# fp32 weight loads on SyncE's queue with on-chip conversion, and a new loop order, in a windowed-attention and highway-FFN kernel

## The chip, the core and the metric

One core of a Trainium2 chip runs the whole kernel. The metric is the time of one execution on the device, in microseconds (us); lower is better. A profile describes one execution; its span is about 2 us shorter than that execution's time. Each variant was timed in alternation with the kernel before on the same chip. The chips differ from round to round, and the median of the kernel before with them (129.19 to 129.88 us), so variants of different rounds are compared by their ratio to it.

## The reference

Attention with 4 sink keys and a causal window of 128, then a highway layer over the concatenated heads (cut):

```python
# q, k, v: (4, 8, 768, 64) fp32, n_sink = 4, window = 128
scores = scale * np.matmul(q, k.transpose(0, 1, 3, 2))
keep = (pos[None, :] < n_sink) | ((rel >= 0) & (rel < window))
scores = np.where(keep, scores, -1000000000.0)
a = softmax(scores)                          # written out in the reference
x = (a @ v), heads joined                    # (3072, 512)
H = np.maximum(x @ w_h, 0.0)                 # w_h, w_t: (512, 512) fp32
T = 1.0 / (1.0 + np.exp(-(x @ w_t + b_t)))
out = T * H + (1.0 - T) * x                  # (3072, 512) fp32
```

## The kernel before

The 3072 tokens are 24 blocks of 128; six blocks make a sequence. For each block the kernel

- loads q, k and v with GpSimd's DMA queue, which casts fp32 to fp16 on the way (rows of 64 elements, so 1,024 packets of 128 bytes for each load),
- transposes q and k on TensorE (`pe_T`) and copies them to SBUF on ScalarE (`act_T`, tile `qk`),
- computes scores (`pe_S`), exponentials on ScalarE (`act_S`), masks on VectorE (`dve_mask`), the product with v (`pe_A`), its reciprocal and scaling on VectorE (`dve_rec`, `dve_x`),
- transposes x on TensorE (`pe_X`), copies it on ScalarE (`act_X`), and does the two FFN products (`pe_Mt` for t, `pe_Mh` for h), `act_u`, and three VectorE steps (`dve_d`, `dve_e`, `dve_o`), followed by the store.

Each engine works through its own instructions in program order, and waits on semaphores for the others. The loads at the head of the program:

```python
def load_w(w, sb):
    nc.gpsimd.dma_start(out=sb, in_=w.rearrange("(kc p) of -> p kc of", p=P))   # casts

with tc.manual_schedule(engines={ENG.Pool}):
    load_qk(0)
    # ... ident (cut)
    load_v(0)
    load_qk(1)
    # ... masks (cut)
    load_v(1)
    load_sink_v(0)
    load_w(moe_w_t, wt_sb)
    load_w(moe_w_h, wh_sb)
    # ... bm (cut)
    load_qk(2)
    load_v(2)
    load_qk(3)
```

The start and the loop (cut):

```python
if i == -2:
    warm_up(8); more_constants(); pe_T(0); act_T(0)
elif i == -1:
    pe_S(0, 0) ...; dve_mask(0, 0); dve_mask(0, 1)
    pe_T(1); act_T(1)
    pe_A(0); dve_rec(0); dve_x(0)
    pe_S(1, 0) ...; dve_mask(1, 0); dve_mask(1, 1)
    pe_X(0); act_X(0); spare(3)
    pe_A(1); dve_rec(1); dve_x(1) ...
elif i == 0:
    pe_Mt(0); act_u(0); pe_X(1); act_X(1); pe_Mt(1)
    pe_Mh(0); dve_d(0); act_u(1)
    pe_T(2); act_T(2)
    ...
else:                                   # the loop
    pe_T(i + 2); act_T(i + 2)
    dve_mask(i, 1); dve_e(i - 2)
    pe_S(i + 1, 0); pe_S(i + 1, 1)
    pe_X(i - 1); act_X(i - 1); act_S(i + 1, 0); dve_o(i - 2)
    pe_A(i); dve_rec(i); dve_x(i)
    # ... sink scores of every other block (cut)
    act_S(i + 1, 1)
    pe_Mh(i - 1); dve_d(i - 1); pe_Mt(i - 1); act_u(i - 1)
    dve_mask(i + 1, 0)
```

The PSUM tiles of `pe_T`, `pe_X`, `pe_Mt`, `pe_Mh` and the sink scores share two buffers in turn, so the order of these steps also decides who waits for whose buffer.

The softmax here doesn't subtract the row's maximum and nothing guards it: scores larger than these inputs give would overflow.

## Time and profile before

| | before |
|---|---|
| median of the runs | 129.77 us |
| span of the profiled run | 127.8 us |
| first qk copy (block 0) starts | 6.90 us |
| block 1's av product done | 15.23 us |
| block 4's av product done | 35.35 us |
| six blocks of the loop | 26.1 us |

"av product done" is read here, and everywhere below, as the start of the reciprocal that follows it on VectorE.

From the page of the kernel before: the head, and busy time of an engine with its share of the span and its count of instructions.

```profile
span 127.8 us, 3253 instructions
...
PE 110.1 (86%) x1315; PEld 67.9 (53%) x1315; DVE 101.8 (80%) x214; ACT 97.6 (76%) x129; POOL 74.9 (59%) x98
```

No engine is the bottleneck over the whole span, so the reading goes by stages. The chain of work that ended last, for the kernel before; columns are start, duration (us), and what it was:

```profile
7.71 0.57 POOL vd L127
8.28 0.76 POOL wt_sb L135
9.04 9.43 DMA wh_sb<-in_moe_w_h_dram
18.47 0.28 issue
18.75 0.87 POOL qsd L86
...
21.38 0.84 POOL qsd L86
22.22 6.38 DMA ksd<-in_k_dram
28.60 0.05 issue
28.64 0.41 PE tp L199 x4
...
69.86 1.04 PE hps L341 x4
70.89 0.22 PE tps L326
71.11 0.88 PE tps L328 x4
71.99 0.02 issue
72.01 0.60 ACT u L334
72.61 0.90 ACT qk L204
73.51 0.49 ACT xT L318
```

Up to 28.6 us the chain holds load issues and loads: the casting h load, then a k load behind it. After that it is a ring: h and t products on TensorE, then u, qk and xT on ScalarE, which the next h product needs. One turn is 4.2 us.

### The profile page before, as it was taken

The page shows a single profiled execution, that of the slowest core. Times are in us where ns is not written, and L with a number is a line of the kernel's source. Part 1 is how long each engine was busy: PE and PEld are TensorE (multiplying, and loading weights), DVE is VectorE, ACT ScalarE, POOL GpSimd, SP SyncE. Part 2 cuts the span into 40 slices and gives each one's busy share as a digit, 9 for nine tenths or more (in the row PEclk, how much of TensorE's full clock was granted, in tenths as well). Part 3 has the DMA queues.
Part 4 walks back from the last instruction along what each step waited for, and adds up shares of the span by engine and source line. Part 5 has one row for each costly group of instructions (what it writes and reads, how often), then busy time and mean ns, then how long its engine had stood idle before and what let it go on. Part 6 is the DMA issues. An engine that isn't in the chain of part 4 may idle for free.

```text
span 127.8 us, 3253 instructions
## 1 busy us (share of the span) xinstructions
PE 110.1 (86%) x1315; PEld 67.9 (53%) x1315; DVE 101.8 (80%) x214; ACT 97.6 (76%) x129; POOL 74.9 (59%) x98
## 2 busy tenths in 40 slices
PE   6758989569999899999998999999989999999620
PEld 2236434447755574586555656755655666564300
DVE  6544626495999898998998998989989999899760
ACT  4066435999897998998987989989969989893310
POOL 6999939999899989999999995005000000000000
PEclk9999999999999999999999999999999999999996
DMA  0999999999999999999999999922022202210222
GB/s 1 105 126 140 165 153 157 180 181 197 160 156 204 204 180 201 163 199 200 164 199 194 208 159 205 186 95 82 8 82 82 82 5 82 82 60 28 82 82 82
DMA packets 79728, 17.00 MB, mean 133 GB/s; under 512 B 75617, under 2 KB 76641, under 8 KB 79714
## 3 DMA queue, kind: packets, MB, share of 16 engines
q0 software_dynamic: 76256, 10.51, 122.6%
q1 hardware_dynamic: 3458, 6.30, 13.3%
q8 instruction: 10, 0.16, 0.5%
q14 instruction: 4, 0.03, 0.1%
HBM read 21.01 MB, written 6.29 MB: 214 GB/s over the span
## 4 chain that ended last, share of the span: by engine, by line
PE 39%; ACT 29%; DMA 12%; POOL 9%; DVE 6%; issue 3%; POOLq 0%; ACTq 0%
PE tps L328 14%; PE hps L341 11%; ACT qk L204 10%; DMA wh_sb<-in_moe_w_h_dram 7%; ACT u L334 6%; ACT e L252 6%; ACT xT L318 5%; DMA ksd<-in_k_dram 5%; PE tps L326 4%; POOL qsd L86 3%; PE sps L244 3%; PE av L280 2%; POOL ksd L87 2%; POOL v L94 2%; PE xtp L313 2%
## 5 line engine op out<-in xcount | busy, mean ns | idle before, releaser
L252 ACT ACTIVATE e<-sps,ebias 128x1024 f16<-128x1024 f32 (+1 forms) x48 | 48.6, 1054 | 1.8 <-PE sps L244 1.8
L263 DVE TENSOR_TENSOR e<-e,mask 128x1024 f16<-128x1024 f16 (+1 forms) x48 | 29.1, 640 | 4.7 <-ACT e L252 4.6
L204 ACT COPY qk<-tp 128x1024 f16<-128x1024 f16 x24 | 24.2, 1009 | 6.4 <-PE tp L199 6.4
L341 PE MATMUL hps<-wh_sb,xT 128*128 128x512 f16 x96 | 24.8, 380 | 3.4 <-ACT xT L318 2.9
L334 ACT ACTIVATE u<-tps 128x512 f16<-128x512 f32 x24 | 14.3, 597 | 16.0 <-PE tps L328 16.0
L328 PE MATMUL tps<-wt_sb,xT 128*128 128x512 f16 x96 | 25.0, 384 | 0.1
L86 POOL DMA_DIRECT2D qsd<-in_q_dram x24 | 22.4, 932 | 3.4 <-DMA wh_sb<-in_moe_w_h_dram 2.0
L94 POOL DMA_DIRECT2D v<-in_v_dram x24 | 22.3, 929 | 0.5 <-DVE dd L347 0.3
L347 DVE SCALAR_TENSOR_TENSOR dd<-hps,xh 128x512 f16<-128x512 f32 x24 | 16.6, 691 | 7.4 <-PE hps L341 5.7
L87 POOL DMA_DIRECT2D ksd<-in_k_dram x24 | 22.1, 920 | 0.5 <-PE tps L328 0.3
L353 DVE SCALAR_TENSOR_TENSOR ee<-u,dd 128x512 f16<-128x512 f16 x24 | 16.5, 689 | 3.5 <-ACT u L334 3.2
L280 PE MATMUL av<-v,e 128*128 128x66 f16 x352 | 17.7, 197 | 0.6 <-DVE e L263 0.5
L328 PEld LDWEIGHTS <-xT 128*128 128x128 f16 x96 | 9.4, 98 | 15.0 <-issue 4.1
L299 DVE TENSOR_TENSOR xh<-av,rec 128x512 f16<-128x512 f32 x24 | 16.6, 692 | 0.8
L359 DVE SCALAR_TENSOR_TENSOR otok<-xh,ee 128x512 f32<-128x512 f16 x24 | 16.6, 692 | 0.8
L280 PEld LDWEIGHTS <-e 128*128 128x128 f16 x352 | 15.2, 100 | 2.2 <-DVE e L263 1.9
L244 PE MATMUL sps<-qk 64*128 64x128 f16 x352 | 14.6, 223 | 1.5 <-ACT qk L204 1.5
L318 ACT COPY xT<-xtp 128x512 f16<-128x512 f16 x24 | 14.4, 598 | 0.4 <-PE xtp L313 0.3
L341 PEld LDWEIGHTS <-xT 128*128 128x128 f16 x96 | 7.9, 97 | 12.0 <-ACT xT L318 5.7
L244 PEld LDWEIGHTS <-qk 64*128 64x128 f16 x352 | 10.4, 97 | 4.8 <-ACT qk L204 1.4
L199 PE MATMUL tp<-ident,ksd 128*128 128x128 f16 x96 | 9.8, 227 | 1.7 <-DMA ksd<-in_k_dram 1.6
L197 PEld LDWEIGHTS <-qsd 128*128 128x128 f16 x96 | 7.2, 100 | 6.8 <-DMA qsd<-in_q_dram 2.2
(51 smaller groups left out, 100.2 us busy)
## 6 DMA issues: line engine op xcount, KB each, us to landing
out_dram<-otok SPq DMA_DIRECT2D x24, 256.0 KB, 4.5
qsd<-in_q_dram POOLq DMA_DIRECT2D x24, 128.0 KB, 6.5
ksd<-in_k_dram POOLq DMA_DIRECT2D x24, 128.0 KB, 6.5
v<-in_v_dram POOLq DMA_DIRECT2D x24, 128.0 KB, 6.7
wt_sb<-in_moe_w_t_dram POOLq DMA_DIRECT2D x1, 512.0 KB, 7.3
wh_sb<-in_moe_w_h_dram POOLq DMA_DIRECT2D x1, 512.0 KB, 9.4
vd<-in_v_dram POOLq DMA_DIRECT2D x4, 4.0 KB, 4.9
bt<-in_moe_b_t_dram SPq DMA_DIRECT2D x1, 2.0 KB
```

The source lines that it names most:

```text
L86: nc.gpsimd.dma_start(out=qsd, in_=q[b, :, rows, :].transpose([1, 0, 2]))
L87: nc.gpsimd.dma_start(out=ksd, in_=k[b, :, rows, :].transpose([1, 0, 2]))
L94: nc.gpsimd.dma_start(out=vt[:, :, 0:D], in_=v[b, :, rows, :].transpose([1, 0, 2]))
L204: nc.scalar.copy(out=qk, in_=tp_of.pop(n))
L244: nc.tensor.matmul(sps[:, hh, o:o + P], lhsT=kk[rows, hp, :], rhs=qT[rows, hp, :], start=True, stop=True)
L252: nc.scalar.activation(out=e.rearrange("p a b c d -> p a (b c d)"), in_=sps[:, :, 0:2 * np_ * P], func=AF.Exp, bias=ebias, scale=SCALE)
L263: nc.vector.tensor_tensor(out=ev, in0=ev, in1=m.unsqueeze(1).to_broadcast([P, 4, np_ * P]), op=ALU.mult)
L280: nc.tensor.matmul(av[:, g, 2 * hl + hh, 0:_AVN], lhsT=e[:, hh, hl, pc, :], rhs=vt[:, 65 * h:65 * h + _AVN], start=first, stop=False, skip ...
L318: nc.scalar.copy(out=xT, in_=xtp_of.pop(n))
L328: nc.tensor.matmul(tps, lhsT=xT[:, kc, :], rhs=wt_sb[:, kc, :], start=False, stop=(kc == NOC - 1))
L334: nc.scalar.activation(out=u, in_=t_of.pop(n), func=AF.Tanh)
L341: nc.tensor.matmul(hps, lhsT=xT[:, kc, :], rhs=wh_sb[:, kc, :], start=(kc == 0), stop=(kc == NOC - 1))
```

## The change

The intent, as the diff shows it: free GpSimd's queue of the weights, give the DMA engines large packets for them, convert on engines that wait at the start anyway, and open the ring by moving the x transpose to the head of the iteration. The diff, cut to its core:

```diff
-    vs_dn = [const.tile([NS4, D], FP16, ...) for i in range(2)]
+    vs_dn = [const.tile([NS4, D], FP32, ...) for i in range(B)]
+    w32 = {w: const.tile([P, NOC, DM], FP32, ...) for w in "th"}
-    with tc.manual_schedule(engines={ENG.Pool}):
+    with tc.manual_schedule(engines={ENG.Pool, ENG.SP}):
+        for w, src in (("t", moe_w_t), ("h", moe_w_h)):
+            nc.sync.dma_start(out=w32[w], in_=src.rearrange("(kc p) of -> p kc of", p=P))
+        nc.sync.dma_start(out=bt32, in_=moe_b_t.unsqueeze(0))
+        for b in range(B):
+            nc.sync.dma_start(out=vs_dn[b], in_=v[b, :, 0:NSINK, :])
         load_qk(0)
 ...
-        load_sink_v(0)
-        load_w(moe_w_t, wt_sb)
-        load_w(moe_w_h, wh_sb)
 ...
             if i == -2:
                 warm_up(8)
                 more_constants()
+                for kc in range(NOC):
+                    convert(nc.scalar, "t", kc)
                 pe_T(0)
                 act_T(0)
 ...
-                pe_T(1)
-                act_T(1)
                 pe_A(0)
                 dve_rec(0)
                 dve_x(0)
+                pe_T(1)
+                act_T(1)
 ...
+            elif i == 0:
+                pe_X(0)
+                act_X(0)
+                convert(nc.vector, "h", 0)
+                convert(nc.vector, "h", 1)
                 dve_mask(1, 0)
                 dve_mask(1, 1)
-                pe_X(0)
-                act_X(0)
-                spare(3)
+                convert(nc.vector, "h", 2)
+                convert(nc.vector, "h", 3)
+                pe_T(2)
+                act_T(2)
                 pe_A(1)
                 dve_rec(1)
                 dve_x(1)
+                pe_Mt(0)
+                act_u(0)
+                pe_Mh(0)
+                dve_d(0)
 ...
+            elif not late:                    # the new loop
+                (no sinks:) pe_X(i-1); act_X(i-1)      (sinks: act_sink(i))
+                dve_mask(i, 1)
+                pe_S(i+1, 0); act_S(i+1, 0); pe_S(i+1, 1)
+                dve_e(i-2)
+                (sinks:) pe_X(i-1); act_X(i-1)
+                pe_T(i+2); act_T(i+2)
+                dve_o(i-2)
+                pe_A(i); dve_rec(i)
+                dve_mask(i+1, 0); act_S(i+1, 1)
+                dve_x(i)
+                pe_Mh(i-1); dve_d(i-1); pe_Mt(i-1); act_u(i-1)
+                pe_sink(i+1)
```

The diff also moves the loads of blocks 10 and 11 by a step in GpSimd's queue. **T0**: the first qk copy (`act_T(0)`). **T1**: block 1's transposes, now behind block 0's av product instead of ahead of it.

More of the change, by code (lines that the diff above doesn't have):

```diff
@@ L113 @@
     vs_bd = [const.tile([P, H, 65], FP16, tag=f"vs{i}", name=f"vs{i}") for i in range(2)]
-    vs_dn = [const.tile([NS4, D], FP16, tag=f"vd{i}", name=f"vd{i}") for i in range(2)]
+    vs_dn = [const.tile([NS4, D], FP32, tag=f"vd{i}", name=f"vd{i}") for i in range(B)]
+    w32 = {w: const.tile([P, NOC, DM], FP32, tag=f"w32{w}", name=f"w32{w}") for w in "th"}
     es_t = [const.tile([P, 2, P], FP16, tag=f"es{i}", name=f"es{i}") for i in range(2)]
@@ L124 @@
             init_v(vt)
-    def load_sink_v(b):
-        nc.gpsimd.dma_start(out=vs_dn[b % 2], in_=v[b, :, 0:NSINK, :])
     def sink_v(b, eng):
         eng.tensor_tensor(
-            out=vs_bd[b % 2][0:NS4, :, 0:D], in0=vs_dn[b % 2].unsqueeze(1).to_broadcast([NS4, H, D]),
+            out=vs_bd[b % 2][0:NS4, :, 0:D], in0=vs_dn[b].unsqueeze(1).to_broadcast([NS4, H, D]),
             in1=bm[0:NS4, :].unsqueeze(2).to_broadcast([NS4, H, D]), op=ALU.mult)
-    def load_w(w, sb):
-        nc.gpsimd.dma_start(out=sb, in_=w.rearrange("(kc p) of -> p kc of", p=P))
-    with tc.manual_schedule(engines={ENG.Pool}):
+    with tc.manual_schedule(engines={ENG.Pool, ENG.SP}):
[4 more added lines that the diff above has]
+            nc.sync.dma_start(out=vs_dn[b], in_=v[b, :, 0:NSINK, :])
         load_qk(0)
@@ L162 @@
         load_qk(3)
-    nc.sync.dma_start(out=bt32, in_=moe_b_t.unsqueeze(0))
     def more_constants():
@@ L366, in lag @@
     def lag(n):
-        if n < 2:
-            return 1 - n
+        if n == 1:
+            return 0
         return 1 if n not in XBAR else 3 if n < LATE else 2
@@ L377, in spare, with convert @@
             nc.tensor.matmul(w, lhsT=warm[:, 0:P], rhs=warm, start=True, stop=True)
+    def convert(eng, w, kc):
+        sb = {"t": wt_sb, "h": wh_sb}[w]
+        if eng is nc.scalar:
+            eng.copy(out=sb[:, kc, :], in_=w32[w][:, kc, :])
+        else:
+            eng.tensor_copy(out=sb[:, kc, :], in_=w32[w][:, kc, :])
     with tc.manual_schedule(engines={ENG.PE, ENG.DVE, ENG.Activation, ENG.SP, ENG.Pool}):
         for i in range(-2, NB + 2):
-            ms = [m for m in range(2, NB) if m + lag(m) == i]
+            ms = [m for m in range(1, NB) if m + lag(m) == i]
             os_ = [m for m in range(1, NB) if m + lag(m) == i - 1]
+            late = len(XBAR) and i > XBAR[0]
             if i == -2:
@@ L411 @@
                 dve_x(1)
+                pe_Mt(0)
+                act_u(0)
+                pe_Mh(0)
+                dve_d(0)
                 sink_ones()
                 sink_v(0, nc.vector)
-            elif i == 0:
-                pe_Mt(0)
-                act_u(0)
+            elif i == 1:
                 pe_X(1)
                 act_X(1)
-                pe_Mt(1)
-                pe_Mh(0)
-                dve_d(0)
-                act_u(1)
-                pe_T(2)
-                act_T(2)
-                dve_e(0)
-                pe_Mh(1)
-                dve_o(0)
-                dve_d(1)
-            elif i == 1:
                 pe_S(2, 0)
                 act_S(2, 0)
-                dve_mask(2, 0)
+                dve_e(0)
                 pe_S(2, 1)
@@ L435 @@
                 act_T(3)
+                dve_o(0)
                 act_S(2, 1)
-                pe_sink(2)
-                act_sink(2)
-            else:
+                dve_mask(2, 0)
+                pe_Mh(1)
+                dve_d(1)
+                pe_Mt(1)
+                act_u(1)
+                dve_mask(2, 1)
+                pe_sink(2)
+            elif not late:
+                sk = has_sink(i)
+                x = on(i - 1) and i > 2
+                if x and not sk:
+                    pe_X(i - 1)
+                    act_X(i - 1)
+                if sk:
+                    act_sink(i)
+                if i > 2 and on(i):
+                    dve_mask(i, 1)
+                if on(i + 1):
+                    pe_S(i + 1, 0)
+                    act_S(i + 1, 0)
+                    pe_S(i + 1, 1)
+                for o in os_:
+                    dve_e(o)
+                if x and sk:
+                    pe_X(i - 1)
+                    act_X(i - 1)
                 if on(i + 2):
@@ L442 @@
                     act_T(i + 2)
-                if on(i):
-                    dve_mask(i, 1)
-                for o in os_:
-                    dve_e(o)
-                if on(i + 1):
-                    pe_S(i + 1, 0)
-                    pe_S(i + 1, 1)
-                if on(i - 1) and i - 1 not in XBAR and i - 1 > 1:
-                    pe_X(i - 1)
-                    act_X(i - 1)
-                if on(i + 1):
-                    act_S(i + 1, 0)
                 for o in os_:
@@ L459 @@
                     dve_rec(i)
+                if on(i + 1):
+                    dve_mask(i + 1, 0)
+                    act_S(i + 1, 1)
+                if on(i):
+                    dve_x(i)
+                if i in XBAR:
+                    sp_X(i)
+                for m in ms:
+                    pe_Mh(m)
+                    dve_d(m)
+                    pe_Mt(m)
+                    act_u(m)
+                if has_sink(i + 1):
+                    pe_sink(i + 1)
+            else:
+                if i == XBAR[0] + 1:
+                    dve_mask(i, 1)
+                    if has_sink(i):
+                        act_sink(i)
+                if on(i + 2):
+                    pe_T(i + 2)
+                    act_T(i + 2)
+                for o in os_:
+                    dve_e(o)
+                if on(i + 1):
+                    pe_S(i + 1, 0)
+                    act_S(i + 1, 0)
+                    pe_S(i + 1, 1)
+                if on(i - 1) and i - 1 not in XBAR:
+                    pe_X(i - 1)
+                    act_X(i - 1)
+                if on(i):
+                    pe_A(i)
+                    dve_rec(i)
+                for o in os_:
+                    dve_o(o)
+                if on(i):
                     dve_x(i)
@@ L474 @@
                     dve_mask(i + 1, 0)
+                    dve_mask(i + 1, 1)
             if on(i + 2) and (i + 2) % NSC == 0:
@@ L479 @@
                     sink_v(b, nc.gpsimd)
-                if b + 1 < B:
-                    load_sink_v(b + 1)
-            for n in {-2: range(3, AHEAD + 1), 0: [], 1: [10, 11]}.get(i, [i + 2 + AHEAD]):
+            for n in {-2: range(3, AHEAD + 1)}.get(i, [i + 2 + AHEAD]):
                 if n < NB:
```

## The prediction

> **What bounds the kernel now.** Two stages.
>
> *Start, 0 to 28.6 us: loads.* The chain of waits runs through GpSimd's DMA issues (0.9 us each), 9.43 us of the wh load, then 6.38 us of a k load. Only at 28.64 us can block 5 be transposed; later the chain holds no load. Beside the casting weight loads, q, k and v loads took 8.0 us to land (3.6 to 4.1 earlier); GpSimd once waited 2.03 us for wh.
>
> *Loop, 28.6 to 118 us: a ring through the engines.* In the timeline an iteration takes 4.20 us, or 4.67 with sink scores: 26.1 us per six blocks. The table of stretches has TensorE busy 24.9 of these, VectorE 23.9, ScalarE 23.8. The ring: TensorE's h and t matmuls (2.1 us), ScalarE's u, qk, xT (2.0), h again. So a perfect order would save at most about 1.2 us per six blocks, 3.6 in 18.
>
> **What the change does.** It removes two casting weight loads (1.5 us of GpSimd; about 7.7 us of DMA). It adds 2 MB of fp32 on SyncE's queue, four ScalarE conversions *ahead of the first qk copy*, four on VectorE where it is idle, and drops three spare matmuls.
>
> The Trainium skill, "DMA: Bandwidth & Descriptors" (queues, rings and completion order), says that each DMA engine takes turns between queues packet by packet. The trace agrees: during a store (25 to 26 us) the software queue moved 636 packets in 1 us instead of about 1,220, the store about 217 GB/s; alone, stores run near 400. Estimate: wt lands near 6.3 us, wh near 11; q and k of block 0 at 5.4 and 7 (before 4.96 and 6.26); k of block 5 near 22 instead of 28.6. Loads stop being the limit.
>
> But the conversions (estimate 4 x 0.5 us, from ScalarE's 128x512 copies) follow wt's landing: the first qk copy starts near 8.4 us instead of 6.90. Walking the new order from there with the trace's durations, block 4's av matmuls end at 34.8 to 36.5 us (before 35.3): early data is spent on a later, more serial start (block 1's transposes wait for block 0's av), partly at the cold matmul rate (427 ns per 128x512, not 216). Start: 0 to +1 us.
>
> *Loop.* The ScalarE ring opens: x is copied first, 2 us before h needs it. But dd now follows rec, mask and xh on VectorE, and the next x transpose needs the buffer that dd frees: 0.04+0.24+0.60+0.61+0.65 = 2.14 us after av, plus 2.04 us of TensorE = 4.18 us. Nearly the old period (4.63 with sink scores); only the half-size block of each sequence gets shorter, about 0.5 us. Over 18 iterations -1.5 us (range -4 to +1). Tail: unchanged within 0.4 us.
>
> Sum near -0.7; the walk leaves out slack that blocks lend each other, so -1.4.
>
> **Predicted: 128.3 us, range 125.3 to 131.0. Faster by over 2%: 0.31; within 2%: 0.58; slower by over 2%: 0.11.**
>
> **What shows it.** Right: weights land near 6 and 11 us; no load in the chain after 12 us; the qk copy starts at 8 to 9 us after four conversions; block 4's av ends near 35.5; iterations of 4.1 to 4.25 us with TensorE waiting for dd. Wrong: qk copy before 7.5 or after 10; average period still 4.35, or below 4.2.
>
> **What would make it wrong.** Weights starved by small packets (wt after 9 us), or delaying q and k; the matmul clock cold to 20 us or more; earlier masks letting all engines fill (period 4.15: about 126); conversions over 0.6 us.

## The result, and the profile after

| | before | after | difference |
|---|---|---|---|
| median of the runs | 129.77 us | 134.03 us | |
| ratio of the fast runs | | 1.034 (95%: 1.030 to 1.038) | slower |
| span of the profiled run | 127.8 us | 132.5 us | +4.7 |
| first qk copy starts (T0) | 6.90 | 11.81 | +4.9 |
| from T0 to block 1's av | 8.33 | 10.09 | +1.8 |
| from T0 to block 4's av | 20.12 | 18.12 | -2.0 |
| from block 4's av to block 22's (18 blocks) | 78.25 | 78.10 | -0.2 |
| from block 22's av to the end | 14.2 | 14.4 | +0.2 |

A ratio is the mean time of one kernel's fast runs over that of the other's of the same rounds, so it is not quite the ratio of the medians. The whole loss lies before block 4. The loop is as long as it was.

The same lines of the page of the changed kernel:

```profile
span 132.5 us, 3280 instructions
...
PE 109.2 (82%) x1312; PEld 68.2 (51%) x1312; DVE 102.3 (77%) x218; ACT 99.7 (75%) x133; POOL 70.6 (53%) x92
```

The chain that ended last, for the changed kernel, columns as before:

```profile
1.33 1.06 POOL qsd L86
2.39 8.72 DMA ksd<-in_k_dram
11.11 0.05 issue
11.16 0.62 PE tp L194 x4
11.78 0.02 issue
11.81 1.02 ACT qk L199
...
75.70 0.88 PE tps L323 x4
76.58 0.02 issue
76.60 0.25 ACT u L329
76.85 0.25 issue
77.09 0.58 ACT xT L313
77.67 1.02 ACT e L247
78.69 0.91 ACT qk L199
79.60 0.04 issue
79.64 0.38 PE tps L321
80.02 0.86 PE tps L323 x4
```

The start now hangs on the very first k load, which took 8.7 us to land where it took 3.8 before; the first q load took 9.0 us instead of 3.6. The view of the k tile for that load, before and after:

```profile
DMA to landing us min/median/max: 3.8/3.8/3.8
...
DMA to landing us min/median/max: 8.7/8.7/8.7
```

The ScalarE conversions, for which the prediction delayed T0, ran from 6.58 to 8.75 us, and ScalarE then waited 3 us more for k. What the DMA engines did meanwhile is in the DMA view of the changed kernel over four stretches, 3 to 4, 6 to 7, 8 to 9 and 10 to 11 us. q1 is SyncE's hardware queue (the weights), q0 GpSimd's software queue (q, k, v); after each name stand packets, MB and the packets' time as a share of 16 engines (over 100% where packets overlap).

```profile
q1 hardware_dynamic: 192, 0.39, 105.0%
...
q1 hardware_dynamic: 166, 0.34, 96.2%
q0 software_dynamic: 30, 0.00, 5.8%
...
q1 hardware_dynamic: 194, 0.23, 78.5%
q0 software_dynamic: 294, 0.04, 57.5%
...
q0 software_dynamic: 1228, 0.16, 243.4%
```

The first q load was issued by 2.4 us and needs 1,024 packets. While the weights were under way, it got almost none: its first packet moved at 5.98 us (3.09 in the kernel before), and by 9 us the software queue had moved 427. In the loop the ring closed again in another place: the t product needs the PSUM buffer that the qk copy frees, and on ScalarE the qk copy comes behind u, xT and one exponential. That turn is 4.32 us (75.70 to 80.02).

The table of stretches for the changed kernel, 8 to 28 us; per stretch the busy time of each engine with its count, then the granted TensorE clock, the DMA share and GB/s:

```profile
8.00:12.00 4.00, 1.22 (x8) 0.69 (x8) 0.41 (x1) 0.95 (x3) 0.00 (x0) 0.50 2.12 183
12.00:16.00 4.00, 1.92 (x23) 1.50 (x24) 1.29 (x4) 2.08 (x3) 3.00 (x6) 0.50 1.62 103
16.00:20.00 4.00, 2.79 (x33) 2.10 (x31) 2.19 (x4) 2.92 (x3) 4.00 (x6) 0.50 1.81 116
20.00:24.00 4.00, 3.62 (x23) 1.78 (x24) 2.54 (x5) 1.82 (x4) 4.00 (x5) 0.50 2.22 144
24.00:28.00 4.00, 3.43 (x37) 2.00 (x36) 2.81 (x7) 2.99 (x5) 4.00 (x6) 0.92 2.30 144
```

TensorE had nothing to do from 4.6 to 10.4 us, and its clock stood at half from 8 to 24 us. The kernel before started at the half rate too (its four k transposes took 0.61 us at 6.26 us and 0.40 at 20.24), but left it earlier, near 16.5 us. Two lines of TensorE's timeline, block 0's t product in the changed kernel and block 1's in the kernel before (start, duration in us, then what it was; x4 stands for four matmuls):

```profile
21.83 1.91 PE L323 MATMUL tps<-wt_sb,xT 128*128 128x512 f16 x4
...
18.19 1.04 PE L328 MATMUL tps<-wt_sb,xT 128*128 128x512 f16 x4
```

The granted clock of a view must be read with care here. In several traces the clock has no record before it turns to full, and the view then counts that time as full: order_only shows 1.00 from 20 to 24 us, yet its block 0's t product at 21.69 us took 1.77 us. So a run's mean clock does not say how long its start ran at half; the length of the matmuls does.

### The profile page after: what moved, and what is told of

Same layout as the page of the kernel before. It is cut to its first block, busy times and chain, and to the rows that moved or that the text cites. A ratio compares the mean times of both kernels' runs of the same rounds, so it can differ in the third digit from the quotient of the medians.

```text
span 132.5 us, 3280 instructions
## 1 busy us (share of the span) xinstructions
PE 109.2 (82%) x1312; PEld 68.2 (51%) x1312; DVE 102.3 (77%) x218; ACT 99.7 (75%) x133; POOL 70.6 (53%) x92
## 4 chain that ended last, share of the span: by engine, by line
PE 51%; ACT 28%; DMA 7%; DVE 7%; issue 4%; POOL 1%; POOLq 0%
PE tps L323 15%; ACT e L247 9%; PE hps L336 9%; ACT qk L199 9%; DMA ksd<-in_k_dram 7%; ACT xT L313 5%; PE tps L321 5%; PE av L275 5%; PE sps L239 4%; ACT u L329 4%; PE tp L192 3%; PE tp L194 3%; PE sk L217 3%; PE xtp L308 3%; PE av L281 2%
## 5 line engine op out<-in xcount | busy, mean ns | idle before, releaser
L247 ACT ACTIVATE e<-sps,ebias 128x1024 f16<-128x1024 f32 (+1 forms) x48 | 50.2, 1051 | 1.2 <-PE sps L239 1.2
L258 DVE TENSOR_TENSOR e<-e,mask 128x1024 f16<-128x1024 f16 (+1 forms) x48 | 31.1, 647 | 7.1 <-ACT e L247 6.9
L336 PE MATMUL hps<-wh_sb,xT 128*128 128x512 f16 x96 | 25.3, 386 | 1.4 <-ACT xT L313 1.3
L323 PE MATMUL tps<-wt_sb,xT 128*128 128x512 f16 x96 | 25.5, 389 | 0.0
L323 PEld LDWEIGHTS <-xT 128*128 128x128 f16 x96 | 9.5, 98 | 17.3 <-issue 7.7
L294 DVE TENSOR_TENSOR xh<-av,rec 128x512 f16<-128x512 f32 x24 | 16.5, 686 | 0.1
L192 PE MATMUL tp<-ident,qsd 128*128 128x128 f16 x96 | 10.1, 231 | 6.0 <-DMA qsd<-in_q_dram 5.8
L313 ACT COPY xT<-xtp 128x512 f16<-128x512 f16 x24 | 13.8, 574 | 1.4 <-PE xtp L308 1.3
L336 PEld LDWEIGHTS <-xT 128*128 128x128 f16 x96 | 8.4, 99 | 9.8 <-ACT xT L313 3.1
L239 PEld LDWEIGHTS <-qk 64*128 64x128 f16 x352 | 10.4, 97 | 4.9 <-ACT qk L199 1.4
L208 POOL COPY ks<-qk 64x16 f16<-64x16 f16 x8 | 2.5, 319 | 19.1 <-ACT qk L199 18.9
```

Of the source, the lines that this page charges most:

```text
L239: nc.tensor.matmul(sps[:, hh, o:o + P], lhsT=kk[rows, hp, :], rhs=qT[rows, hp, :], start=True, stop=True)
L247: nc.scalar.activation(out=e.rearrange("p a b c d -> p a (b c d)"), in_=sps[:, :, 0:2 * np_ * P], func=AF.Exp, bias=ebias, scale=SCALE)
L258: nc.vector.tensor_tensor(out=ev, in0=ev, in1=m.unsqueeze(1).to_broadcast([P, 4, np_ * P]), op=ALU.mult)
L313: nc.scalar.copy(out=xT, in_=xtp_of.pop(n))
L323: nc.tensor.matmul(tps, lhsT=xT[:, kc, :], rhs=wt_sb[:, kc, :], start=False, stop=(kc == NOC - 1))
L336: nc.tensor.matmul(hps, lhsT=xT[:, kc, :], rhs=wh_sb[:, kc, :], start=(kc == 0), stop=(kc == NOC - 1))
```

## The experiments

The first theory was: the loads lose everything (weights queued first hold back q and k), the order is neutral. Its rivals: the order loses it, or the conversions do. All 18 variants gave correct results. The table sums them up; times of the one profiled run in us, ratio of the fast runs against the kernel before in the same rounds.

| variant | T0 | block 1's av | block 4's av | median | ratio |
|---|---|---|---|---|---|
| before | 6.90 | 15.23 | 35.35 | 129.77 | 1 |
| changed kernel | 11.81 | 21.90 | 40.02 | 134.03 | 1.034 |
| order_only | 7.17 | 21.51 | 39.23 | 133.95 | 1.031 |
| loads_only | 12.23 | 20.49 | 38.99 | 132.54 | 1.020 |
| convert_late | 12.06 | 22.19 | 41.37 | 135.68 | 1.045 |
| gate_k0 | 7.25 | 21.89 | 39.54 | 134.02 | 1.033 |
| order_T2late | 6.80 | 16.54 | 35.94 | 131.46 | 1.017 |
| old_gate_k1 | 6.86 | 15.23 | 39.81 | 133.67 | 1.031 |
| new_gate_k1_T2late | 7.29 | 17.14 | 40.58 | 135.98 | 1.051 |
| warm_first | 11.64 | 20.91 | 37.27 | 133.28 | 1.018 |
| new_split | 8.88 | 21.48 | 40.15 | 133.83 | 1.036 |
| old_split | 8.65 | 16.49 | 35.17 | 129.48 | 1.002 |
| old_split_warm | 8.65 | 16.51 | 35.18 | 129.05 | 0.998 |
| before_warm | 6.79 | 15.04 | 35.34 | 129.68 | 1.003 |
| after_T2late | 12.08 | 22.18 | 42.13 | 135.74 | 1.044 |
| new_split_T2late | 8.96 | 18.80 | 38.99 | 133.41 | 1.025 |
| after_T1early | 12.14 | 21.00 | 38.33 | 133.17 | 1.026 |
| new_split_T1early_T2late | 8.88 | 16.91 | 36.56 | 131.24 | 1.009 |
| pool_free (flawed) | 12.07 | 22.16 | 45.74 | 139.08 | 1.069 |
| old_half_t_warm (flawed) | 7.34 | 15.19 | 45.69 | 139.49 | 1.074 |

### order_only and loads_only: each half alone

order_only is the changed kernel with the old loads:

```diff
-        for w, src in (("t", moe_w_t), ("h", moe_w_h)):
-            nc.sync.dma_start(out=w32[w], ...)
+        load_w(moe_w_t, wt_sb); load_w(moe_w_h, wh_sb)     # where they stood before
-                    convert(...)                           # all eight
```

> The new loop order with the old loads (weights cast by GpSimd's queue, no conversions). Theory (the loads cost the time, not the order): the loop takes 26.1 us per six blocks as in both kernels; the start is again limited by the loads, block 4's av matmuls end at 35 to 36 us, time 129.5 to 130.5 us. Rival (the new order is the cause, through the more serial start or the freed buffers): 133 us or more.

Measured 133.95 us, ratio 1.031. The theory fell: the order alone loses as much as the whole change. The waits of order_only up to 30 us (engine and line, what it waited for, us in total, times, longest) say where:

```profile
PE tp L196 <- DMA qsd<-in_q_dram: 4.9, 2, 4.7
```

T0 was at 7.17 us, nearly as before. But TensorE reached T2 with q and k of block 2 still behind the casting weight loads; k landed at 19.9 us. Behind T2 in TensorE's queue stood block 1's av product and block 0's FFN, both ready to run. They are what TensorE did in the kernel before until block 2's loads had come.

loads_only has the old order with the new loads and conversions:

```diff
+        (weights first on SyncE's queue, as in the changed kernel)
             if i == -2:
+                for kc in range(NOC):
+                    convert(nc.scalar, "t", kc)
                 pe_T(0)
 ...             (the old start and loop otherwise; h converted around dve_mask(1, *))
```

> The new loads and conversions in the old order. Theory: q and k of block 0 land at 10.4 and 11.2 us as in the changed kernel, the first qk copy starts at about 11.8 us; the old start order is about 1.7 us shorter up to block 1's av, so 131 to 134 us. Rival (order is the cause): about 129.8 us.

Measured 132.54 us, ratio 1.020, T0 at 12.23 us: as expected. So the loads alone lose too. Alone the parts lose 3.1% and 2.0%, together 3.4%, not 5.1%. They do not add, and that had to be explained.

### convert_late: the conversions as the cause

```diff
-                for kc in range(NOC):
-                    convert(nc.scalar, "t", kc)         # ahead of pe_T(0)
 ...
+                for kc in range(NOC):
+                    convert(nc.scalar, "t", kc)         # ahead of pe_X(0)
```

> The changed kernel with ScalarE's four t conversions moved from ahead of the first qk copy to ahead of the first x copy; loads unchanged. Theory (starved q and k): the first qk copy still starts at about 11.8 us and the time stays 133.5 to 135 us. Rival (my prediction's reason, conversions ahead of the qk copy delay the start): a gain of 1.5 us or more.

Measured 135.68 us. T0 stayed at 12.06, so the conversions did not hold it: the prediction's reason did not bind in the changed kernel. Moved to where ScalarE is needed, they cost about 1.6 us, a little more than the theory allowed. At the head of the queue they were free, because k came later still.

### gate_k0, old_gate_k1: the weights later

gate_k0 is convert_late with the weights issued after k of block 0 has landed. The wait is made by data: a one-column copy from that k into the weight tile, which the load then overwrites.

```diff
+            nc.vector.tensor_copy(out=w32[w][:, 0, 0:1], in_=qk_sd[0][1][:, 0, 0:1])
+            nc.sync.dma_start(out=w32[w], ...)          # for t and h, now here
```

> As convert_late, and the two weight loads are issued only after k of block 0 has landed (a one-column VectorE copy from that k into each fp32 weight tile, which the load then overwrites). Theory (weights queued first starve q and k): q and k of block 0 land at 5.0 and 6.3 us as in the kernel before, the qk copy starts at 6.9, block 4's av ends at 35 us, time about 129 us (128 to 130.5), 4 to 5 us less than the changed kernel. Rival (the lost time lies in order or conversions): 133 us or more.

T0 came at 7.25 us, as expected: the weights ahead of q and k are what delayed it. But the time was 134.02 us, which was the rival's number. The starvation only moved: q and k of block 1 now came late (its qk copy at 14.74 us), and T2 waited for k of block 2 until 20.3 us. The first theory was incomplete, and was changed to: two holds on the same stretch, the weights' place in the DMA order and T2's place in TensorE's order, each enough by itself.

old_gate_k1 has the old order, and the weights wait for k of block 1:

```diff
+            nc.vector.tensor_copy(out=w32[w][:, 0, 0:1], in_=qk_sd[1][1][:, 0, 0:1])
+            nc.sync.dma_start(out=w32[w], ...)
 ...             (t converted behind act_X(0), h behind dve_x(1))
```

> Old order with the fp32 weights on SyncE's queue, issued only once k of block 1 has landed, the conversions placed where ScalarE and VectorE wait (after block 0's x copy; after block 1's x). Theory (the weights being first in the engines' queues is all that the new loads lose): block 0's and 1's qk copies start at 6.9 and 10 us as in the kernel before, time 129 to 130.5, some 2.5 us below loads_only's 132.5. Rival (fp32 weights and conversions cost time wherever they stand): 131.5 or more.

Measured 133.67 us: missed. Blocks 0 and 1 came as in the kernel before (T0 6.86, block 1's av 15.23). Then the t weights, issued at 9.67 us, landed only at 17.9, 8.2 us after their issue instead of 5.7, and block 0's t product waited for them. The DMA view of this run from 10 to 11 and from 16 to 17 us, columns as above, shows how the two queues share:

```profile
q0 software_dynamic: 930, 0.12, 184.2%
...
q1 hardware_dynamic: 160, 0.32, 92.2%
q0 software_dynamic: 145, 0.02, 28.0%
```

The weights' first packet moved 1.8 us after their issue (1.2 us in the changed kernel, with nothing beside them). Later the two queues move packets in nearly equal numbers: 160 of 2 KB beside 145 of 128 bytes, and in the same way 153 beside 152 in gate_k0 (14 to 15 us) and 151 beside 152 in new_split (15 to 16 us). By the shares of time above, a packet of 2 KB took about 92 ns and one of 128 bytes about 31, so with equal turns the software queue falls from about 1,220 packets per us alone to an eighth of that. The Trainium skill, "DMA: Bandwidth & Descriptors" (section on queues, rings and completion order), says that an engine takes turns between queues at packet granularity. The counts agree with equal turns, though they cannot tell single packets from runs of equal length. What they add is the unequal time of a turn. At times the software queue got less: 30 packets beside 166 in the changed kernel from 6 to 7 us, and 10 beside 167 in gate_k0 from 10 to 11. Why is not settled.

### order_T2late, new_gate_k1_T2late: T2 moved back

```diff
-                pe_T(2)
-                act_T(2)
                 pe_A(1)
                 dve_rec(1)
                 dve_x(1)
                 pe_Mt(0)
                 act_u(0)
                 pe_Mh(0)
                 dve_d(0)
+                pe_T(2)
+                act_T(2)
```

> New loop order with the old loads, but block 2's qk transposes and copy stand behind block 0's h matmuls instead of ahead of block 1's av matmuls; nothing else differs from order_only. Theory (what the order loses is head-of-line blocking: TensorE's queue held block 1's av and block 0's FFN behind a transpose whose k landed at 19.9 us): block 1's av ends at 16.5 to 17.5 us (21.5 in order_only), block 4's at 35.5 to 37, time 129.5 to 131.5, so 2.5 us or more below order_only. Rival (the serial start or the loop's order itself costs the time): within 1 us of order_only's 133.95.

In order_T2late (old loads) the time fell from 133.95 to 131.46 us, and block 1's av from 21.51 to 16.54, as expected. Each against the kernel before of its own rounds, the loss of the medians went from 4.3 to 2.25 us: T2's place is about 2 of the 4.3 us that the order loses with the old loads. At block 4's av it is 3.3 of 3.9 us (39.23, 35.94, and 35.35 before). In the profiled run of order_T2late the 18 blocks from there to block 22's av took 1.0 us longer than in the kernel before, and the rest 0.6 us; these two are not traced.

> The changed kernel with both repairs: weights gated on k of block 1, conversions moved into waits, block 2's transposes behind block 0's h matmuls. Theory (two separate losses, each enough by itself, which is why gate_k0 alone gained nothing): both vanish, time 129.5 to 131 us. Rival (the loop order costs): 132.5 or more.

Measured 135.98 us: missed, and the slowest of these. It has late weights as old_gate_k1 has, so it tells little about the order. It does show that gating 2 MB on block 1 lost with either order.

### warm_first: the clock

```diff
-                warm_up(8)
+                warm_up(34)
-                pe_A(0)
+                pe_A(0, warm_n=3)
-                pe_A(1)
+                pe_A(1, warm_n=2)
```

> The changed kernel with 34 instead of 8 warm-up matmuls and 5 more while TensorE waits for the first masks; it should hold the full clock from about 5 us until the loads have come. If the half-rate clock from 8 to 24 us (mean granted clock 0.928 in the changed kernel) is a part of the loss, block 1's av ends 1 us earlier or more and the time falls to about 133; if the start is bound by ScalarE and by waits, the time stays within 0.5 us of 134.0.

Two of four runs took 131.44 and 131.84 us; the other two took 134.73 and 135.93, have no kept trace, and are left unexplained. The ratio in the table uses the two fast ones, the median all four. In the profiled fast run the clock stood at full from 6 us, T0 was hardly earlier (11.64), and block 4's av came at 37.27 us instead of 40.02. So in that execution the half clock is up to 2.7 us of the changed kernel's loss, after T0. One profile is thin evidence for the size, and whether the fillers hold the clock is not settled. The Trainium skill, "TensorE: Matmul & The Clock Gate" (Part 1), says that the array's clock falls to half after an idle window of about 3.4 us and that it takes such a window of work to get it back. The changed kernel agrees with the fall (last warm-up matmul over at 4.6 us, half clock by 8). How much work brings the clock back is not shown: TensorE worked from 10.4 us on, with gaps, and the full rate came only near 24.7.

### new_split and old_split: half of the bytes first

Only t is queued first (1 MB); h waits for k of block 1, and VectorE converts it behind block 1's x.

```diff
+        nc.sync.dma_start(out=bt32, ...)
         nc.sync.dma_start(out=w32["t"], ...)
 ...
+        nc.vector.tensor_copy(out=w32["h"][:, 0, 0:1], in_=qk_sd[1][1][:, 0, 0:1])
+        nc.sync.dma_start(out=w32["h"], ...)
```

> The changed kernel, but only the bias and the t weights are queued first; the h weights are issued once k of block 1 has landed, and VectorE converts them after block 1's x. Theory (in the changed kernel the 2 MB queued first hold back q and k of block 0, by about 2.6 us per MB): the first qk copy starts at 8 to 9 us instead of 11.8, block 4's av ends 2.5 to 3.5 us before the changed kernel's 40.0, time 130.5 to 132. If the delay is all or nothing (the software queue starved however few bytes are ahead), the qk copy still starts after 11 us.

T0 moved from 11.81 to 8.88 us, 2.9 us for 1 MB less: the delay goes with the bytes ahead. T0 cannot gain much more here: the conversions, still ahead of it on ScalarE, ended at 8.74 us. This is the floor that the prediction had named (8.4). The time did not move (133.83). T2 waited for q and then k of block 2 until 19.9 us, as TensorE's timeline shows, and block 1's av came at 21.48 us, where it was.

```profile
19.12 0.61 PE L193 MATMUL tp<-ident,qsd 128*128 128x128 f16 x4 [3.02 <-DMA qsd<-in_q_dram]
```

This was the other hold at work (the h weights shared the queue's time with these loads from about 12 us on), but it had not been expected, so the expectation of 130.5 to 132 us was missed.

> Old order with the same split loads as new_split. Theory (compute of the start takes 26.8 us from the first qk copy to block 4's av where no load holds it up, as in loads_only): qk copy at 8 to 8.5 us, block 4's av at 34.5 to 35.5 us, time 128 to 130, at or just below the kernel before. If the h weights arrive late as the gated t weights did in old_gate_k1, it is 131 or more.

With the old order the same loads give 129.48 us, ratio 1.002, block 4's av at 35.17: as expected. The new kind of load costs nothing if few of its bytes stand ahead of q and k and if TensorE has other work while k of block 2 comes. It gains nothing either.

### old_split_warm and before_warm: does the clock bound the old order?

```diff
-                warm_up(8)
+                warm_up(18)                      # 14 in before_warm
-                pe_S(0, 0)
+                pe_S(0, 0, warm_n=4)             # likewise pe_A(0) 2, pe_S(1, 0) 3
```

> old_split with 18 warm-up matmuls instead of 8 and 9 more in places where TensorE waits for copies and masks. If the half-rate clock costs the start 1 to 3 us (as warm_first's two fast runs suggest), this is 1 us or more below old_split and the fastest so far, 126 to 128.5; if not, it equals old_split.

> The kernel before with 14 warm-up matmuls and the same 9 fillers, loads unchanged. The start of the kernel before is bound by loads up to 28.6 us, so a warm clock should gain little: within 1 us of 129.3. A gain of 1.5 us or more would say that the clock and not the loads bounds its start.

old_split_warm took 129.05 us (0.998, interval 0.996 to 1.001) and before_warm 129.68 (1.003): neither gains. Block 4's av stood still in both (35.18 and 35.34). In these two starts the clock did not bound block 4's av.

### after_T2late and new_split_T2late: completing the table

The edit is that of order_T2late, on the changed kernel and on new_split.

> The changed kernel with block 2's qk transposes and copy moved behind block 0's h matmuls, loads unchanged (2 MB of weights first). In the changed kernel these transposes hardly waited (block 0's q and k came so late that k of block 2 was there). Theory (two alternative holds): no gain, within 0.7 us of 134.0. Rival (the place of the transposes costs by itself, as in order_only): 131.5 to 132.5.

> new_split with the same move. In new_split the transposes waited for k of block 2 until 19.9 us, 3 us of TensorE waiting. Theory (two alternative holds; here both are loosened): block 1's av ends at 17 to 18 us (21.5 in new_split), block 4's av at 36 to 37.5, time 130 to 131.5, 2.5 us or more below new_split and the changed kernel. Rival: 133 or more.

after_T2late brought no gain, and rather a loss, past what was expected: 135.74 us (ratio 1.044, interval 1.037 to 1.051, against 1.030 to 1.038 of the changed kernel), with block 2's qk copy at 26.62 instead of 20.57. With q and k of block 0 that late, k of block 2 was there in time, and moving T2 back only delayed it. So the right place of T2 depends on when its loads land. new_split_T2late brought block 1's av from 21.48 to 18.80 us, but the ratio only from 1.036 to 1.025: the total, 133.41 us, missed the expected 130 to 131.5. Something else in the order still held the start.

### after_T1early and new_split_T1early_T2late: the other serial step

```diff
+                pe_T(1)
+                act_T(1)
                 pe_A(0)
                 dve_rec(0)
                 dve_x(0)
-                pe_T(1)
-                act_T(1)
```

> The changed kernel with block 1's qk transposes and copy put back ahead of block 0's av matmuls; nothing else. Theory (serial start as the prediction named it): block 1's qk copy at about 14.7 us instead of 16.4, block 1's av at 20.3 to 20.7 instead of 21.9, time 132.3 to 133.2. Rival (that time is taken up by the next wait, block 2's loads, which land at 19.2 us): within 0.5 us of 134.0.

> new_split_T2late with the same step undone too. Theory (three causes make up the loss: bytes queued first, and two serial steps of the start): block 1's av at 16.5 to 17 us as in old_split, block 4's at 36 to 37, time 130 to 131.5. Rival (the new order loses elsewhere in the start): 132.5 or more.

after_T1early: 133.17 us, block 1's qk copy at 14.82 instead of 16.38, block 4's av at 38.33 instead of 40.02. The gain of 0.9 us in the medians is small (ratio 1.026 with an interval from 1.019 to 1.033, against 1.034 in other rounds), though its place is the expected one. The second is clearer at block 1's av, 1.9 us earlier than in new_split_T2late: with all three steps undone (bytes first, T1, T2) the time is 131.24 us against new_split_T2late's 133.41 (ratio 1.009 against 1.025), block 1's av at 16.91 and block 4's at 36.56. In both runs the clock came back earlier as well (about 22 us in after_T1early and 19 in the second, against 24.7 in the changed kernel), so a part of the gain behind block 1 can be the clock's. The second stays 1% above the kernel before. What remains of it, 1.2 us at block 4, is not traced further.

### pool_free and old_half_t_warm: two flawed runs

In the changed kernel GpSimd waited 5.0 us for the first qk copy (it copies the sink keys out of it) before it could issue block 2's loads. pool_free takes this copy later:

```diff
+            if i == 0:
+                pool_sink(0)
             if on(i + 2) and (i + 2) % NSC == 0:
                 b = (i + 2) // NSC
-                pool_sink(b)
+                if b:
+                    pool_sink(b)
```

> The changed kernel with GpSimd's copy of block 0's sink keys taken two steps later in its queue, so that GpSimd's next load issues do not wait 5 us for the first qk copy. Theory (the wait is hidden: block 2's loads are not yet needed when they land): within 0.5 us of 134.0. Rival (the late issue of block 2's and 3's loads is part of the loss): 133 or less.

Measured 139.08 us, because of the edit's own fault: the copy now stood behind some twenty load issues, ran at 30.67 us, and the sink scores of block 2 waited for it. Up to there the run is usable. Block 1's av came at 22.16 us (21.90 in the changed kernel), the second x copy at 25.15 (25.38). With GpSimd free the start was not faster, so that 5 us wait was hidden up to 25 us; for the whole kernel the run decides nothing.

old_half_t_warm was meant to beat the kernel before: the old order, 512 KB of t first, the rest gated on k of block 1, the same GpSimd edit, and the warm-up fillers.

```diff
+        nc.sync.dma_start(out=w32["t"][:, 0:2, :], ...)
 ...
+                nc.vector.tensor_copy(out=w32["t"][:, 2, 0:1], in_=qk_sd[1][1][:, 0, 0:1])
+                nc.sync.dma_start(out=w32["t"][:, 2:4, :], ...)
+                (then h in the same way)
```

> Old order, built from the findings: only half of t (512 KB) is queued first, the rest of t and h once k of block 1 has landed; half of the t conversions on VectorE early, half on ScalarE behind the first x copy; GpSimd's sink copy later; warm-up matmuls as in old_split_warm. Theory: q and k of block 0 land at 5.3 and 6.8 us, the first qk copy at 7 to 7.5 us, block 4's av at 33.5 to 35 us, time 127 to 129, below the kernel before. If the second half of t arrives late, as in old_gate_k1, it is 130 or more.

Measured 139.49 us, with the same fault (7.8 us of TensorE waiting for the sink keys). Before that fault, T0 came at 7.34 us as expected, and the second half of t held up block 0's t product by 2.4 us. No version beat the kernel before; old_split_warm equals it.

## Why the prediction was wrong, point by point

- **The step that failed:** "Estimate: wt lands near 6.3 us, wh near 11; q and k of block 0 at 5.4 and 7". wt landed at 6.5 and wh at 9.6, but q at 10.3 and k at 11.1. What failed is the overlap of the two queues: the small packets of q and k did not move beside the weights, but for the most part after them. The prediction had listed it among the things that would make it wrong ("or delaying q and k") and not priced it. The estimate rested on one microsecond of the kernel before, given here from its DMA view, 25 to 26 us:

```profile
q0 software_dynamic: 636, 0.08, 125.0%
q1 hardware_dynamic: 106, 0.20, 51.6%
```

  As far as its numbers show, it was read as a split that lasts. It is a mean over a store of only 128 packets and the time in which the software queue ran alone. With the pair of old_gate_k1 (160 and 145 per us), 106 store packets fill 0.66 us and let about 96 small ones through; the other 0.34 us at 1,220 add about 410, together about 510 of the 636 measured. At the shared rate of old_gate_k1, 145 per us, q's 1,024 packets would need 7 us. The changed kernel did worse than that rate while the weights moved: the software queue moved one packet before 6 us and 427 before 9, then 1,063 from 9 to 10 us. Why it started 2.9 us later than in the kernel before is not settled.
- **"The first qk copy starts near 8.4 us"**, because the conversions precede it: it started at 11.81, and not for that reason (convert_late, and the 3 us that ScalarE waited after its conversions). This is the mis-sized term: 3.4 us, of a total missed by 5.7.
- **"Loads stop being the limit"**: false for the first load, true later in the changed kernel.
- **"A later, more serial start (block 1's transposes wait for block 0's av), partly at the cold matmul rate"**: right in direction. The walk allowed 26.4 to 28.1 us from T0 to block 4's av; 28.2 was measured. after_T1early and new_split_T1early_T2late bear out the serial step; warm_first puts up to 2.7 us on the clock in one execution, which stayed at half to 24 us in the changed kernel. The prediction had listed this as a risk ("the matmul clock cold to 20 us or more") and not priced it.
- **T2** was not seen as a cost at all. In the changed kernel it is not one, since the late start hides it; with the loads repaired it takes what the repair gains (new_split; in gate_k0 together with the late k of block 1).
- **The loop, "-1.5 us"**: -0.2 measured. The ring did open where the prediction said and closed at another shared buffer: in the chain the t product waits for the qk copy, with a turn of 4.32 us where 4.18 was predicted. "TensorE waiting for dd" was not seen in the chain.
- **The tail, "unchanged within 0.4 us"**: +0.2, right.

Why the halves do not add: both are waits of TensorE in the same stretch for the same DMA engines. Late q and k of block 0 hide the wait of T2; early ones expose it. That rests on order_only, new_split, gate_k0 and after_T2late together.

## What to carry to other kernels

In these runs a queue of large packets did not run beside a queue of small ones as an equal. Before moving bulk loads to the front on a second queue, count the small packets that the first computation needs, and price them at one for one against the bulk packets at best. When a repair moves the first event and not the total, look for a second hold on the same stretch: here the in-order engine that reached an instruction whose load was late, with ready work behind it. Do not take a sharing rate from a window that is longer than the burst in it.

## What the Trainium skill lacked or had wrong

- "DMA: Bandwidth & Descriptors" (queues, rings and completion order) gives turns per packet but not what follows from unequal packets: beside 2 KB packets, the queue of 128-byte packets fell from 1,220 to 145 per us (160 large ones beside them).
- No page was found that has the late start of a queue beside a busy one: with the weights under way the software queue's first packet moved at 5.98 us in the changed kernel, against 3.09 in the kernel before, for an issue at the same time (1.3 us).
- "TensorE: Matmul & The Clock Gate" (Part 1) says "the ramp penalty is <1% of a typical kernel span". Here the half clock from 8 to 24 us goes with up to 2.7 us at block 4's av, 2% of the span, in the one profiled execution that held the full clock (warm_first). In the kernel before the page's figure holds: with the fillers it took 1.003 of its time (before_warm).
